# Two steps of the first expert group and the last block's sums taken into the group's switch

## The chip, the cores and the metric

The kernel runs on one core of one Trainium2 chip. The core has five engines with instruction streams of their own: TensorE (PE in the profile, with its weight loads as PEld), VectorE (DVE), ScalarE (ACT), GpSimd (POOL) and SyncE (SP, which only issues transfers). Matrix products read SBUF and write PSUM; the other engines read PSUM and write SBUF; transfers between device memory and SBUF go through 16 DMA engines. Instructions of an engine run in their order; engines wait for each other by semaphores. The metric is the device time of one execution in microseconds (us).

## The reference

It is an attention layer followed by a layer of experts, all in float32. The attention has 4 sequences of 768 tokens, 8 heads of 64. A query sees the first 8 keys and the last 96, with a bias that falls with distance. Each of the 3072 tokens of 512 values then goes to one of 8 experts:

```python
logits = x @ w_gate
expert_idx = np.argmax(logits, axis=1)
...
for e in range(E):
    mask = expert_idx == e
    xe = x[mask]
    h = np.maximum(xe @ w1[e], 0.0)     # 512 -> 1024
    ye = h @ w2[e]                      # 1024 -> 512
    out[mask] = gate_w[mask, None] * ye
```

How many tokens an expert gets depends on the data.

## The kernel before, in words

The kernel has two stages. **Attention** goes through 24 blocks of 128 queries (`steps(n)`, N = 24). It is pipelined over blocks: the step of block n computes its scores, while the values of block n-1, the sums (softmax denominators and gate logits) of block n-2 and the final rows of block n-3 are made. So the last blocks leave a tail behind the loop: `values_part(N)` and `sums_part(N)`, and then `sums_part(N + 1)` for the last block of all. A `sums_part` is 12 small products (L571), four transposes (L578), a copy on ACT (L573) and one more transpose (L581). The rows of the tokens, with gate and number, are scattered by GpSimd into device memory, sorted by expert.

**Experts**: the groups run in the order 0, E, 1, 2, ... 7. Group 0 is expert 0 with the tokens of the first three sequences only, so that it can start before the last sequence is routed; group E holds expert 0's tokens of the last sequence, computed by plain products (L1026). A group reads its tokens in two halves (even and odd slots) and multiplies in Winograd's way: seven products of quarter size in place of eight, as seven steps. The up product has two such sevens (`ups`, 14 steps), the down product one. Sums of quarters are made by DVE ahead (`x_sums`, L847 to L850, `w_sums`, `h_sums`) and behind each step (for example L915). A float32 product appears in the profile as two weight loads and two passes (MATMUL).

The number of columns of the products depends on how many tokens the group has. `SIZES` lists the column counts for which code exists, up to 256. `tables` compares the group's count with the list and leaves an index in SBUF. TensorE's code for a group stands once for every entry of the list (a form); the other engines' code stands once. Three things choose the form:

TensorE's code is brought by DMA (queue q8 in the profile).

Everything is recorded in program order by `Flow`, which works out the semaphores; no scheduler moves instructions later. In a group's code, `run(steps, first)` calls the steps and, after step i, what `at_(i, ...)` has put there for the other engines. In group 0, `ups[:1]`, `sums_part(N + 1)` and `ups[1:2]` are recorded ahead of `with f.forms(...)`, so they stand once, with 256 columns; from `ups[2:]` on everything is within the forms. The form's index for group 0 is loaded in the last attention step (L1239), ahead of the last transpose of its sums; the hint is recorded after the loop (L1322).

## Time and profile before

| What | us |
|---|---|
| Time, median of 3 runs (496.9 to 499.92) | 497.37 |
| The profiled execution, its own time | 498.01 |
| Its span, first to last instruction | 496.1 |
| TensorE busy, products | 473.4 |
| DVE busy | 355.8 |
| Hint of group 0, last instruction | 158.8 |
| Branch into group 0's form | 165.9 |
| Branch out of it | 196.3 |
| Branch into group 1's form | 217.2 |

The last four rows are moments from the span's start. The span is what the profile covers; 1.9 us of the execution lie outside it. Busy times are sums over the span and overlap between engines. In the profile's rows, a line number is the kernel's line that issued the instruction; "128x176" behind a product of L883 means 128 partitions and 176 columns. The granted clock of TensorE was full from 6.9 us to the end of the work (mean 0.989).

### The profile page before, as it was taken

Reading aid. Unit: us, or ns where it says so; the run is one execution under the profiler, and the core shown is the slowest. Engines: PE = TensorE matmul, PEld = TensorE weight load, DVE = VectorE, ACT = ScalarE, POOL = GpSimd, SP = SyncE. Lnnn points to the kernel's source line nnn. Section 1 sums busy time; section 2 is a strip of 40 time slices with the busy share of each in tenths; the row PEclk is TensorE's granted clock in tenths of the full one; section 3 lists DMA queues with packets and bytes.
Section 4 is the critical chain, followed back from the end, with each engine's and each line's share of the span. In section 5 each row is a group of like instructions: output and inputs, shape, how many; then the busy total and the mean of one; then the engine's idle time right before and its main releaser. Section 6 shows DMA issues by size and latency. Waiting matters only on the chain. (4 is left out here: it accounts for less than half of the span.)

```text
span 496.1 us, 10821 instructions
## 1 busy us (share of the span) xinstructions
PE 473.4 (95%) x4413; PEld 447.9 (90%) x4413; DVE 355.8 (72%) x638; ACT 172.4 (35%) x309; POOL 166.4 (34%) x196
## 2 busy tenths in 40 slices
PE   7999999999998999999999999999999999999990
PEld 7888878887886899899999999999999999999980
DVE  6466777897876884666777886768877776787850
ACT  5665555644654230322114213204214203303410
POOL 2653578567775053302104213204304303003011
PEclk9999999999999999999999999999999999999995
DMA  9999999988624437999808918826936853701000
GB/s 175 216 249 263 194 235 265 251 205 190 153 88 86 171 131 164 204 223 213 187 6 206 286 32 218 235 52 161 269 84 161 256 112 115 210 1 49 21 24 30
DMA packets 120093, 79.26 MB, mean 160 GB/s; under 512 B 86170, under 2 KB 103066, under 8 KB 120020
## 3 DMA queue, kind: packets, MB, share of 16 engines
q1 hardware_dynamic: 112482, 63.52, 57.6%
q0 software_dynamic: 6480, 14.45, 8.2%
q8 instruction: 52, 0.85, 0.8%
q10 hardware_dynamic: 1058, 0.26, 0.3%
q14 instruction: 21, 0.17, 0.1%
HBM read 61.39 MB, written 23.71 MB: 172 GB/s over the span
## 5 line engine op out<-in xcount | busy, mean ns | idle before, releaser
L883 PE MATMUL psum<-arena 128*128 128x208 f32 (+8 forms) x1760 | 286.2, 324 | 0.6 <-DVE arena L915 0.5
L883 PEld LDWEIGHTS psum<-arena 128*128 128x128 f32 x1760 | 280.8, 190 | 2.2 <-issue 0.9
L873 POOL DMA_INDIRECT out_dram<-arena,to x16 | 22.4, 1402 | 169.4 <-ACT arena L867 146.3
L529 DVE TENSOR_TENSOR arena<-psum,arena 128x1024 f32<-128x1024 f32 x40 | 48.4, 1219 | 30.5 <-PE psum L519 30.5
L537 ACT ACTIVATE arena<-arena 128x1024 f32<-128x1024 f32 (+1 forms) x48 | 47.5, 989 | 47.4 <-DVE arena L529 38.4
L543 POOL TENSOR_TENSOR arena<-arena 128x512 f32<-128x512 f32 x40 | 51.8, 1298 | 30.3 <-ACT arena L537 30.0
L907 ACT ACTIVATE arena<-arena 128x512 f32<-128x512 f32 x48 | 30.2, 630 | 61.2 <-DVE arena L939 25.4
L519 PE MATMUL psum<-arena 64*128 64x128 f32 x704 | 46.4, 280 | 1.8 <-ACT arena L505 1.8
L519 PEld LDWEIGHTS psum<-arena 64*128 64x128 f32 x704 | 41.8, 187 | 5.4 <-issue 2.5
L556 PE MATMUL psum<-arena 128*64 128x128 f32 x704 | 43.7, 276 | 0.4 <-issue 0.4
L911 ACT COPY arena<-psum 128x512 f32<-128x512 f32 (+1 forms) x24 | 13.5, 560 | 81.4 <-PE psum L883 81.3
L556 PEld LDWEIGHTS psum<-arena 128*64 128x64 f32 x704 | 37.9, 137 | 3.0 <-issue 0.8
L790 POOL DMA_INDIRECT xg_dram<-small,pad x24 | 23.4, 975 | 50.0 <-ACT arena L920 39.1
L655 POOL DMA_INDIRECT xg_dram<-arena,slot_i x24 | 24.4, 1017 | 21.5 <-DVE arena L978 16.0
L939 DVE TENSOR_TENSOR arena<-arena,psum 128x512 f32<-128x512 f32 x24 | 16.5, 688 | 16.4 <-PE psum L883 13.7
L926 DVE TENSOR_TENSOR arena<-arena,psum 128x512 f32<-128x512 f32 x23 | 15.8, 688 | 17.0 <-PE psum L883 16.2
L978 DVE TENSOR_TENSOR arena<-arena,psum 128x512 f32<-128x512 f32 x23 | 15.8, 688 | 15.4 <-PE psum L883 13.5
L944 DVE TENSOR_TENSOR arena<-arena,psum 128x512 f32<-128x512 f32 x24 | 16.5, 689 | 14.1 <-PE psum L883 12.0
L873 POOL DMA_INDIRECT out_dram<-ylast,to x17 | 17.0, 1001 | 22.0 <-ACT ylast L867 13.9
L739 DVE TENSOR_TENSOR arena<-arena 128x1024 f32<-128x1024 f32 x16 | 20.3, 1266 | 2.8 <-DMA arena<-in_moe_w_dram 2.8
L915 DVE TENSOR_TENSOR arena<-arena,psum 128x512 f32<-128x512 f32 (+1 forms) x24 | 15.8, 656 | 8.3 <-PE psum L883 7.9
L742 DVE TENSOR_TENSOR arena<-arena 128x1024 f32<-128x1024 f32 x16 | 19.5, 1221 | 1.7 <-issue 1.5
(164 smaller groups left out, 551.9 us busy)
## 6 DMA issues: line engine op xcount, KB each, us to landing
arena<-in_moe_w_dram SPq DMA_DIRECT2D x64, 512.0 KB
arena<-xg_dram SPq DMA_DIRECT2D x64, 128.0 KB
arena<-in_v_dram SPq DMA_DIRECT2D x24, 256.0 KB
arena<-in_q_dram SPq DMA_DIRECT2D x23, 256.0 KB
arena<-in_k_dram SPq DMA_DIRECT2D x23, 256.0 KB
xg_dram<-arena SPq DMA_DIRECT2D x2, 1032.0 KB
xg_dram<-arena,slot_i POOLq DMA_INDIRECT x24, 5.9
xg_dram<-small,pad POOLq DMA_INDIRECT x24, 8.7
```

Source lines behind the costliest of these rows:

```text
L519: f.pe.matmul(self.psum[:, 2 * g + a, c:c + P], lhsT=kt[r, m, :], rhs=qt[r, m, :], start=True, stop=True, skip_group_check=True)
L529: f.dve.tensor_tensor(e, s, self.bias[:, g, :, 1:3, :].rearrange("p h k c -> p h (k c)"), ALU.add)
L537: f.act.activation(e, e, AF.Exp)
L543: f.pool.tensor_tensor(self.es[n % 3][:, g], e[:, :, 0:P], e[:, :, P:2 * P], ALU.add)
L556: f.pe.matmul(po[r, m, :], lhsT=self.v[(n - ab) % 6][:, 2 * m + a, :], rhs=self.e[n % 2][:, m // 2, 2 * a + m % 2, P * ab:P * ab + P], sta ...
L655: self.f.pool.indirect_dma_start(out=self.xs[:], out_offset=bass.IndirectOffsetOnAxis(ap=k["slot_i"][:, b % 2, u:u + 1], axis=0), in_=self ...
L739: return [lambda: V.tensor_tensor(c["t3"], c["b22"], c["b12"], ALU.subtract), lambda: V.tensor_tensor(c["t1"], c["b12"], c["b11"], ALU.sub ...
L742: lambda: V.tensor_tensor(c["t4"], c["b21"], c["t2"], ALU.subtract)]
L790: self.f.pool.indirect_dma_start(out=self.xs[:], out_offset=bass.IndirectOffsetOnAxis(ap=self.keep["pad"][:, g, j:j + 1], axis=0), in_=sel ...
L873: return pool.indirect_dma_start(out=self.out[:], out_offset=bass.IndirectOffsetOnAxis(ap=self.keep["to"][:, g, j:j + 1], axis=0), in_=sel ...
L883: f.pe.matmul(self.psum[:, bank, 256 * t + cut.start:256 * t + cut.stop], lhsT=w[k][:, ts(t, 128)], rhs=x[k][:, cut], start=(fresh and t = ...
L907: f.act.activation(d, d, act)
```

## The change

Three edits:

1. The list of sizes: steps of 2 columns begin at 160 instead of 168, and between 208 and 256 there are 220, 232 and 244. That makes 37 forms instead of 32.
2. The first two up steps of group 0 and, between them, the last block's `sums_part(N + 1)` are recorded within the group's forms. The two steps then have the form's column count instead of 256, and the branch comes before them. Each of the 37 bodies of group 0 holds the 12 products and five transposes of the sums and the 8 products of the two steps.
3. The hint for group 0 stands in the last attention step, in the place of the load, and does the load itself (L79: where no load was recorded, it records one). TensorE's order there was load, transpose (L581), hint; it is load, hint, transpose.

```diff
-    RUNS = (range(128, 168, 4), range(168, 208, 2), range(208, 256, 48))
+    RUNS = (range(128, 160, 4), range(160, 208, 2), range(208, 256, 12))
...
             if n == N - 1:
-                f.load(*forms[0])
+                f.hint(*forms[0])
             at.both(n, 0)
...
         assert not numbers and not w0 and not w0_sums and not scat
-        f.hint(*forms[0])
         at.normal(N - 3, U)
...
             if g == 0:
 
-                run(ups[:1], 0)
-                sums_part(N + 1)
-                run(ups[1:2], 1)
                 pieces = ex.w_pieces(1)
...
             with f.forms(*forms[g]):
+                if p == 0:
+                    run(ups[:1], 0)
+                    sums_part(N + 1)
+                    run(ups[1:2], 1)
                 run(ups[2:], 2)
```

## The prediction

> **What bounds the kernel now.** I read the page's busy shares first, then TensorE's products kept apart by shape, then the order of time around the first expert group, then what TensorE's sequencer does there, last the DMA.

> ```profile
> PE 473.4 (95%) x4413; PEld 447.9 (90%) x4413; DVE 355.8 (72%) x638; ACT 172.4 (35%) x309; POOL 166.4 (34%) x196
> ```
> TensorE (PE) works 473.4 of 496.1 us, so whatever shortens or stops its stream moves the end almost one to one; the chain of work that ended last covers only the final 3 us and does not help.

> ```profile
> L883 PE MATMUL psum<-arena 128*128 128x176 f32 x192 | 29.3, 313 | 0.0
> ...
> L883 PE MATMUL psum<-arena 128*128 128x256 f32 x16 | 3.9, 386 | 0.0
> ```
> These are group 0's products: 192 passes at the count that its form chose (176 columns) and only 16 at the full 256. The 16 are the two steps that the change moves.

> ```profile
> 162.13 0.29 PE L581 MATMUL psum<-ident,arena 128*128 128x128 f32 x1
> 162.26 1.89 PE L883 MATMUL psum<-arena 128*128 128x256 f32 x8
> ...
> 164.87 0.69 DVE L848 TENSOR_TENSOR arena<-arena 128x512 f32<-128x512 f32 x1
> ...
> 165.61 4.38 PE L883 MATMUL psum<-arena 128*128 128x256 f32 x24
> ...
> 179.83 19.26 PE L883 MATMUL psum<-arena 128*128 128x176 f32 x128
> ```
> Step one runs from 162.26, step two from 165.61, just after DVE's L848 has made the sum that it reads (165.56). Passes follow each other at (1.89-0.38)/7 = 0.216 us at 256 columns and (19.26-0.31)/127 = 0.149 us at 176.

> ```profile
> L277 PEldq COMPARE_BRANCH  x16: 297/310/642, 165.9 to 482.4; - x16
> ```
> ```profile
> q8 instruction: 52, 0.85, 0.8%
> ```
> ```profile
> 199.00:202.00 3.00, 2.66 (x23) 2.26 (x22) 0.69 (x1) 2.27 (x4) 0.91 (x1) 1.00 1.06 265
> ```
> The first row is the branch into and out of the forms (sixteen, shortest, median and longest in ns). The first branch into a form is at 165.9, behind eight 256-column passes that are queued, so its 0.34 us and the 0.4 us around it cost nothing. Queue q8 brings TensorE's code, 52 packets of 16 KB. The last row (window, then busy time of the five engines, granted clock, DMA share, GB/s): around 200 us the DMA engines are full (share 1.06), which matters below.

> **What it removes.** Two steps of 8 passes go from 0.216 to 0.149 us each: 16 x 0.067 = 1.07 us less. Nothing else of TensorE's work changes: the counts that the other groups run (208, 182, 200, 184, 206, 198, 136) all stand in the new list of 37; the new 220, 232 and 244 are not used. DVE's table (L775) grows from 31 to 36 entries a group: 35 elements more in the larger call, a few hundredths beside products.

> **What it adds at the entry.** The branch now comes right after the transpose at 162.13, with no queue of work behind which to hide. Even with its code present, its sequence took 165.63 to 166.40 before the next product; that would put step one at about 163.1 instead of 162.26, a loss of 0.84.

> But is the code there? The trace's q8 packets here start at 148.80, 159.34, 162.53, 169.07, 183.28 and 201.61 us. From 124.20 to 159.34 TensorE went through 1025 instructions in four packets: 256 a packet. [...] The 159.34 packet belongs to the stream itself: between the third and the fourth of the hint's instructions lies a gap of 0.22 us where 0.06 is usual, so a block ends there, and the next is asked for. The hint ends at 158.89, and its target comes as the next packet, at 162.53, 3.2 us behind (in groups 2 to 7, too, the hint's packet follows the one before by 3.1 to 3.7 us[...]). DMA was idle (0.01 in 157.0 to 162.3), so this isn't contention. When is a block usable? In groups 5 and 7 the branch took 0.62 and 0.64 us instead of 0.31 to 0.41; it ended 1.35 and 1.34 us after its packet did. So here: 162.53 + 1.22 (the packet) + 1.35 = 165.10. Before, the branch came at 165.90 and found it; now it comes at about 162.4 and waits.

> The move of the hint doesn't help: it passes one transpose only (two instructions), the load of its index starts at 157.33 as before, and the block ends at the same place in the stream, now just ahead of the hint itself. The transpose of 158.20 is held behind six hint instructions until about 158.9; DVE's chain (L590 at 158.57, busy without a break up to 166.7) starts 0.7 us later, so L848 ends at 166.26. That would hold step two if the branch were quick; with the stall step two is later than that, and it is covered.

> Sum: first load 0.15 us after the branch (group 7), its product 0.13 later: 165.38, against 162.26: +3.12. The shorter steps give back 1.07, DVE's wait ahead of step two (165.37 to 165.61) another 0.21. Step three begins at 169.28 instead of 167.44: **+1.84 us**. Bounds: the block usable 0.25 sooner or later, 1.6 to 2.1.

> What is queued behind the waiting branch: all of TensorE; ACT's copies; the last block's DVE chain (L590 at 168.25) and with it the scatters on POOL; on SP the four w2 loads (L722 at 165.56) that wait for the last transposes and now go at about 168.2. They serve expert 1's second half, more than 50 us on. SP's loads at 186 to 204 move with the chain.

> **What it adds at the exit.** A product in float32 is two loads and two passes. Group 0's body before: 104 x 4 + 12 bf16 products x 2 + hint + exit branch = 442 instructions, two blocks. Now 8 more products (32), 12 sums (48), 5 transposes (10): 532, three blocks, the third holding 20 instructions. The trace shows that the exit's block is asked for only when the stream enters the block that holds the exit: the 183.28 packet comes with 223 of the body's instructions begun and 34 queued ahead, at number 257, 13 us ahead of the exit branch (196.26). Now this point is number 512. It is passed when 478 have begun, 54 instructions or 27 passes x 0.149 = 4.0 us before the body's end (198.78 + 1.84 = 200.62), at 196.6. From there 0.7 us to the packet (groups 2 to 7 show 0.71 to 0.76 after the entry branch), 1.15 for it and 1.35 until usable: 199.8 if DMA is free, in time. It isn't free: after the old exit (196.57) the next packet began at 201.61, 4.3 us later than 0.7 would give. With that row, usable at 204.1, first load 204.3: **+3.7 us**. Bounds: 0 without contention; 5.1 with the 5.7 that the body packets of groups 2 to 4 lag (some 72 instructions, 36 passes x 0.16, past number 256). I take 3.7, the nearest row in time and load.

> **The clock.** TensorE would stand idle twice for 2.9 and 3.7 us. The granted clock was halved at 484.7, 1.85 us after the last product (482.88), so an idle stretch of this length may halve it. [...] At the start the clock rose 5.4 us after the first product; half of that, 2.7 us a gap, is the upper bound, 0 the lower. I take 0.5 in all[...].

> Total: 1.84 + 3.7 + 0.5 = +6.0. The profiled execution (498.01 us, span 496.1 and 1.9 around it) would be 504.0; the median of the runs, 497.37, becomes **503.4 us**.

> **Rivals.** (1) Not slower. One mechanism: the code for the body arrives by 162.4, because the hint, now at the block's edge, replaces the fetch of 159.34 rather than queueing behind it (159.34 + 0.9 + 1.35 = 161.6). From that point the branch costs only its own 0.84, and L848's 166.26 sets step two: step three at 167.51 instead of 167.44. With the exit hidden too this is 497.4; if DVE's chain is less late, 496.9. [...] Against: in before the hint came 0.2 us after the edge and lost. (2) Entry stall alone, exit hidden behind the 34 queued instructions: +1.84, 499.2. For: free DMA would be in time; against: share 0.98 to 1.14 from 190 to 208. (3) Exit stall alone: 501.1. (4) Both gaps halve the clock at full price: up to 508, the tail.

> **How the numbers follow.** Forecast (both stalls, clock somewhere) 0.56, its own range 500.9 to 506.5; entry alone 0.17; exit alone 0.09; neither 0.14; over 506.5 0.04. The range 498.0 to 506.5 leaves out the case of neither and the tail. About 1% (5.0 us, 502.3) is what a measurement of this kernel tells from no change; the forecast lies just past it. Slower by over 1%: three quarters of the forecast, a fifth of exit alone and the tail, 0.48; faster 0.02; the rest, 0.50, within.

> **What would show it.** Right: the first branch into a form at about 162.4, lasting some 2.7 us; 208 passes at 176 and none at 256 columns; step three about 1.8 us later than 167.44; a code packet more in group 0; an exit branch of several us near 198, with TensorE idle before L861's first transposes; everything behind shifted alike. Wrong: entry branch at 0.3 to 0.4 us (rival 1), or exit at 0.3 us (rival 2), or the shift lost again at a later DMA wait of DVE's (L739 waits 2.8 us in all).

## The result, and the profile after

The kernel after takes 504.37 us, the median of six executions (501.58 to 510.35); the kernel before, timed on the same chip, 497.31 (496.79 to 499.92). The ratio is 1.0127, with an interval of 1.0097 to 1.0157: slower by 1.3%. (A ratio leaves out executions more than 1.5% above their kernel's fastest, here that of 510.35, so it isn't the quotient of the medians beside it.) The forecast was 503.4. The six executions fall into two groups, 501.58, 501.86, 502.73 and 506.01, 508.40, 510.35. The profiled one took 502.73 (span 500.8), so it belongs to the quick group and shows 4.7 us of loss where the medians differ by 7.

The page after, busy time and the queue of TensorE's code; then TensorE's products by shape:

```profile
PE 474.0 (95%) x4413; PEld 448.7 (90%) x4413; DVE 360.1 (72%) x638; ACT 172.3 (34%) x309; POOL 166.8 (33%) x196
...
q8 instruction: 53, 0.87, 0.8%
```
```profile
L883 PE MATMUL psum<-arena 128*128 128x176 f32 x208 | 32.0, 314 | 0.7 <-issue 0.5 <-DVE arena L848 0.2
```

The row had 192 passes before; the 16 of the two moved steps have joined it, none with 256 columns is left, and there is one packet of code more. Yet PE's busy time rose by 0.6 us although 16 passes became shorter: other passes became longer (L861's from 17.8 to 19.4 us in all, L1026's from 14.6 to 15.6). The order of time around the entry (start, length, line, product, count, and in brackets the idle time ahead of it and who ended it):

```profile
162.24 1.45 PE L883 MATMUL psum<-arena 128*128 128x176 f32 x8 [0.53 <-issue]
...
165.39 3.85 PE L883 MATMUL psum<-arena 128*128 128x176 f32 x24 [0.19 <-DVE arena L848]
```

There is no stall at the entry. The branch began at 161.65 and took 0.44 us; one packet of code came between the hint (ended at 157.94) and the branch, at 158.96, one microsecond behind the hint. Step one takes 1.45 us in place of 1.89. Measured from the load of the index (156.55 now, 157.33 before), step one starts 0.76 us later than before, step two 0.56, and the step behind both still 0.02 (166.69 now, 167.44 before). So what the shorter passes give is used up even where nothing stalls: the transpose behind the hint starts 1.44 us after the load in place of 0.88, the branch has no queued work to hide behind, and step two waits for DVE's sum. The exit is different. First the sixteen branches (shortest, median, longest in ns), then the order of time behind the body:

```profile
L277 PEldq COMPARE_BRANCH  x16: 292/350/6149, 161.7 to 487.2; - x16
```
```profile
201.71 3.86 PE L861 MATMUL psum<-ident,arena 128*128 128x128 f32 x16 [3.38 <-DVE arena L739]
...
211.80 0.27 PE L1308 MATMUL psum<-ident,ok 128*1 128x128 f32 x1
```

The longest branch, 6.15 us, is group 0's exit: it began at 195.51 with 34 instructions queued ahead, the last pass started at 198.02, and TensorE stood for 3.38 us. The row names DVE's L739, but such names are inferred, and the branch fits better: it ended at 201.66, 0.05 us ahead of L861, and the last packet of code before that, of 199.15, took 1.13 us. The same two products before:

```profile
198.93 1.04 PE L861 MATMUL psum<-ident,arena 128*128 128x128 f32 x8
...
207.24 0.27 PE L1308 MATMUL psum<-ident,ok 128*1 128x128 f32 x1 [0.34 <-DVE ok L1303]
```

L861's products start 2.78 us later than there, or 3.56 measured from the load. Last, two windows of after (window, length, busy PE, PEld, DVE, ACT, POOL, granted clock, DMA share, GB/s):

```profile
199.00:202.00 3.00, 0.29 (x2) 0.29 (x3) 2.00 (x3) 0.00 (x0) 0.00 (x0) 0.80 1.11 265
202.00:205.00 3.00, 3.00 (x15) 2.54 (x15) 2.52 (x6) 1.61 (x3) 0.61 (x1) 0.50 0.97 149
```

The clock was halved from 200.78 to 207.61. L1308, in group E, comes 4.56 us later than before where L861 came 2.78 later: the halved clock cost 1.78. The account of the 4.7 us of span: attention 0.78 quicker, the body's last pass 0.03 later measured from the load, exit +3.53, clock +1.78, later groups +0.15.

### The profile page after: what moved, and what is told of

The parts are those of the page before. It is cut to its first block, busy times and chain, and to the rows that moved or that the text cites. A ratio compares the mean times of both kernels' runs of the same rounds, so it can differ in the third digit from the quotient of the medians.

```text
span 500.8 us, 10821 instructions
## 1 busy us (share of the span) xinstructions
PE 474.0 (95%) x4413; PEld 448.7 (90%) x4413; DVE 360.1 (72%) x638; ACT 172.3 (34%) x309; POOL 166.8 (33%) x196
## 5 line engine op out<-in xcount | busy, mean ns | idle before, releaser
L883 PE MATMUL psum<-arena 128*128 128x176 f32 (+7 forms) x1760 | 285.3, 323 | 1.3 <-issue 0.5
L883 PEld LDWEIGHTS psum<-arena 128*128 128x128 f32 x1760 | 280.2, 190 | 3.0 <-issue 1.9
L556 PE MATMUL psum<-arena 128*64 128x128 f32 x704 | 43.7, 276 | 0.0
L556 PEld LDWEIGHTS psum<-arena 128*64 128x64 f32 x704 | 37.9, 137 | 2.6 <-issue 0.2
L944 DVE TENSOR_TENSOR arena<-arena,psum 128x512 f32<-128x512 f32 x24 | 16.5, 688 | 14.6 <-PE psum L883 14.5
L861 PE MATMUL psum<-ident,arena 128*128 128x128 f32 x132 | 19.4, 292 | 3.7 <-DVE arena L739 3.4
L740 DVE TENSOR_TENSOR arena<-arena 128x1024 f32<-128x1024 f32 x15 | 21.2, 1413 | 0.0
```

What stands on the lines that cost most here:

```text
L556: f.pe.matmul(po[r, m, :], lhsT=self.v[(n - ab) % 6][:, 2 * m + a, :], rhs=self.e[n % 2][:, m // 2, 2 * a + m % 2, P * ab:P * ab + P], sta ...
L740: lambda: V.tensor_tensor(c["t1"], c["b12"], c["b11"], ALU.subtract),
L861: self.f.pe.transpose(pt[:, c, :], self.yt[:, c, hh, ts(bb, 128)], self.keep["ident"][:])
L883: f.pe.matmul(self.psum[:, bank, 256 * t + cut.start:256 * t + cut.stop], lhsT=w[k][:, ts(t, 128)], rhs=x[k][:, cut], start=(fresh and t = ...
```

## The experiments

Ratios are to the kernel before, timed beside each set of kernels: 499.29 us beside e1 to e4, 498.59 beside e5 to e8, 499.66 beside e9 to e11 and 499.26 beside e12. Stretches within a kernel are from its one profiled execution.

The theory: code comes in blocks of 256 instructions, an estimate from the packets (in after, 1028 instructions of TensorE began in the four packets' time from 123.41 to 158.96), and what decides is where a branch stands in its block. Blocks and edges below are counts by that estimate; no trace shows what a packet holds. By the theory the exit stalls because the stream enters the third block 20 instructions ahead of the exit branch, while DMA is full (share 1.06 in 196 to 199).

**Is it the third block? e4: the kernel before, with its body padded** to 532 instructions by 45 tiny products. Nothing of the change is in it.

```diff
+def pad():
+    pr, oh = psum[:, U, 384:392], keep["oh"][:, 0, :]
+    for _ in range(45):
+        f.pe.matmul(pr, lhsT=before[:], rhs=oh, start=True, stop=True, skip_group_check=True)
...
-at_(4, lambda: at.counts(U, whole), lambda: at.gates(B - 1, whole))
+at_(4, pad, lambda: at.counts(U, whole), lambda: at.gates(B - 1, whole))
```

> The kernel before, with nothing changed but 45 small products (8 columns, bf16) ahead of the counts in group 0's body, whose results the counts overwrite: the body grows from 442 to 532 instructions, as in the change. Theory: the exit stalls as in the change, +3.7 and about +1.6 from the halved clock, and the products cost 45 x 0.025 = 1.1: 503.7 (501 to 507), exit branch 4 to 7 us. Rival (moving the steps and sums is what costs): 497.3 + 1.1 = 498.4, exit branch 0.3 us.

Measured: 503.79 us, ratio 1.0096 (1.0066 to 1.0126). Its branches, and the first work behind the exit:

```profile
L277 PEldq COMPARE_BRANCH  x16: 292/320/6171, 166.0 to 487.8; - x16
```
```profile
203.69 3.50 PE L861 MATMUL psum<-ident,arena 128*128 128x128 f32 x16 [3.40 <-DVE arena L739]
```

6.17 and 3.40 us, as in after (6.15 and 3.38), without any edit of the change: the length of the body alone makes the exit's stall. The body's place in the program does not show in it: counted through the whole program, the exit stands 8 instructions behind a multiple of 256 in e4, 174 in e1 and 214 in after, and its branch took 6.17, 6.26 and 6.15 us.

**Two blocks again, e3**: the change with the last down step of group 0 outside the forms; the body has 500 instructions.

```diff
-run(ex.down(g, (lambda: [...]) if early else None), D)
+downs = ex.down(g, (lambda: [...]) if early else None)
+run(downs[:-1] if p == 0 else downs, D)
+    if p == 0:                      # behind the forms
+        run(downs[-1:], D + 6)
```

> The change with the last step of group 0's down product behind its forms, at 256 columns: the body has 500 instructions, two blocks. Theory: the exit's code is asked for at instruction 256, 13 us ahead; exit branch 0.3 us, no halved clock; the last step costs 16 x 0.067 = 1.07 more. 497.3 + 0 at the entry + 1.07 = 498.4 (497.4 to 499.2). Rival (the loss comes from the move of the sums and the branch, or from transfers that start earlier): still about 504 + 1.

Measured: 510.33 us, ratio 1.023 (1.0187 to 1.0273), 12 us over the expectation. The exit branch took 0.32 us as expected. But group 1's branch into its form, 0.31 us before, took 4.26:

```profile
202.66 1.04 PE L861 MATMUL psum<-ident,arena 128*128 128x128 f32 x8
...
225.76 6.51 PE L883 MATMUL psum<-arena 128*128 128x208 f32 x26 [2.00 <-issue]
```

No idle time ahead of L861, but 2.00 us ahead of group 1's products, and the clock halved for 3.41 us behind it. Thirty-seven bodies that are each 32 instructions shorter shift the code of all later groups by a number that isn't a multiple of 256. Counted through the program, an edge now fell 61 instructions ahead of group 1's branch (189 in the change, 115 in the kernel before), and a packet came at 222.73, behind the branch's start of 221.3. Attention ends 2.6 us later than in before, with waits for the loads of q and k, which the edit doesn't touch. The profiled execution is the quickest of the four (506.03); what the others lost, 4 to 7 us more, no profile shows. So an edit of a form's length also moves every later branch against the edges, and with the exit's stall gone (0.32 us) another stood in the next group (4.26). That the edge made this one is argued from its place, not shown by a run of its own.

**How far ahead, and how full? e5**: the change with the same padding, so that the exit stands 110 instructions into its third block instead of 20.

> The change with 45 tiny products (8 columns, bfloat16, 90 instructions) added to group 0's body ahead of the counts; the body grows from 532 to 622 instructions and its exit from 20 to 110 instructions into the third block. Theory (the exit's block is asked for only when the stream enters the block that holds the exit, and 20 instructions were too few to hide a fetch): now some 10 us lie between, the exit branch takes about 0.3 us, TensorE doesn't idle ahead of L861, and the clock isn't halved there; against the change's quick executions -5.3 us for the exit and its clock, +1.1 for the products, so about 0.3 us over the kernel before, 4 to 6 more in executions in which the entry stalls. Rival (a third block costs a stall wherever the exit stands, or the stall is the cost of leaving a long body): exit still 6 us, total 5 to 6 us over the kernel before.

Measured: 503.79 us (499.39 to 509.11), ratio 1.0072 (1.0045 to 1.01). The profiled execution took 503.16; its entry and what follows the exit:

```profile
166.19 1.86 PE L883 MATMUL psum<-arena 128*128 128x176 f32 x8 [3.43 <-DVE arena L847]
...
204.33 1.04 PE L861 MATMUL psum<-ident,arena 128*128 128x128 f32 x8
```

The exit branch took 2.01 us, not 0.3, but it started 34 queued instructions ahead of the body's end and was over at 203.68, before the last pass started (204.18). So TensorE did not stand and the clock was not halved: the exit costs nothing. The quickest executions, 499.4, are 0.8 over the kernel before; the padding alone is 1.1 (by the end of e4's body, from the load). The rival, any third block costs, falls. The 3.43 us at the entry are the stall that the prediction described and that the profiled execution of the change did not have; the clock was halved behind it (the row's eight passes took 1.86 us, 1.45 in after).

**e6** moves expert 1's first four w1 loads (2 MB) behind the gathers on SP.

```diff
 ex.load_x(E, last)
+ex.load_x(1, last)
 for fn in pieces[:4]:
     fn()
-ex.load_x(1, last)
```

> The change with expert 1's first four w1 loads on SP put behind the gathers of its tokens instead of ahead of them. Theory (the 4.3 us in the exit's packet are the DMA engines, full with these loads): if the loads leave the stretch 196 to 201, the packet comes 1 to 3 us sooner and the exit branch takes 2 to 5 us instead of 6.1; if other transfers fill the stretch, the DMA share there stays at 1.0 and the branch at 6. Rival (the delay is the fetch's own, not contention): 6 us with a DMA share well below 1.

Measured, one execution: 505.06 us.

```profile
203.33 1.09 PE L861 MATMUL psum<-ident,arena 128*128 128x128 f32 x8 [1.68 <-DVE arena L978]
...
214.46 0.27 PE L1308 MATMUL psum<-ident,ok 128*1 128x128 f32 x1 [3.10 <-DVE ok L1303]
```

The exit branch took 4.45 us instead of 6.15. Its packet came 1.85 us after the branch's start; in after, e1, e2, e4 and e7 it came 3.6 to 3.9 after it. So with this order of the transfers the packet came at least 1.75 us sooner after the branch's start. That the w1 loads are the cause is likely but not shown: in seven kernels (after, e1, e2, e4, e7, e9, e10) the exit's packet starts 0.15 to 0.82 us after the last of their 512 packets (in after 199.15 after 198.84), but in e5 and e6 it comes in their midst, and in e6 they run from 196.97 to 209.05, through the fetch. DMA stayed busy (share 1.43 in 196 to 198, 0.84 in 198 to 200), so what the exit costs with idle DMA isn't shown. Nor is the kernel quicker: attention ends 3.3 us later than in after, and L1308 waits 3.10 us, because DVE waits for the moved loads.

**The entry. e1** is the change with the list of 32 sizes as before; **e2** is the change with load and hint back in their old places. The diffs are the change's own lines for `RUNS`, and for `f.load` and `f.hint`, reversed.

> The change with the old list of 32 sizes. Theory (the exit branch of group 0 stands in the first 20 instructions of a third block of code, which is asked for late and while DMA is full): the list plays no part; exit branch of group 0 4 to 7 us, clock halved for some us behind it, 504 us (501.5 to 508). Rival (the longer list, with more code and a larger table, costs): back near 497.5.

> The change with load and hint in their old places (load, transpose, hint). Theory: the hint is then two instructions later, behind the edge of a block again, so that the stream's own next block is fetched first (packet near 158.5 to 159.5) and the form's 3.2 us behind it; the entry branch, at about 161.7, waits until about 164.4 and takes 2.5 to 3 us instead of 0.44. With the exit stall as in the change: about 2 us more than it, 506. Rival (the code is there by 162 wherever the hint stands): entry branch 0.4 us, time as the change, 504.

Measured: e1 508.14 us (504.61 to 511.64), ratio 1.0143 (1.0078 to 1.0209); e2 509.61 (509.10 to 513.60), ratio 1.0198 (1.0165 to 1.0232). In both profiled executions the entry stalls, and the exit as well (6.26 and 6.37 us). e1's first product:

```profile
167.60 2.71 PE L883 MATMUL psum<-arena 128*128 128x176 f32 x8 [3.73 <-DVE arena L848]
```

The entry branch took 3.64 us in e1, 3.50 in e2, 3.34 in e5, and 0.43 or 0.44 in after, e3, e6 and e10, with the hint, by the count, one to three instructions behind the block's edge in all seven profiled executions. In the three that stall, the last packet of code ahead of the branch's end starts 1.0 to 1.1 us after the branch does; that it holds the form's code, asked for only when it was missed, is inferred from its time. In the four others a packet follows the hint itself by a microsecond. In the trace of before, two packets came ahead of the branch, at 159.34 and at 162.53; in e4, whose code up to this branch is that of before, with the hint at the same moment (158.75, 158.84 in before), one packet alone came, at 159.89, and the branch took 0.34. The busy share of the DMA engines in tenths, from 158 to 162 us in slices of 0.1 us, first of before, then of e4:

```profile
DMA  0000000000000500000000000000000000000000
```
```profile
DMA  0000000000000000005000000000000000000000
```

So the packets differ between executions of the same code, two in the one and one in the other. That the stream's own next block and the hint's target change places in them is the author's reading.

e1 and e2 also lost at a place that no theory had named: group 5's branch took 3.58 and 3.02 us. By the count, an edge lies 9 and 29 instructions ahead of it there; with 29 it took 0.83 us in after.

**Does the hint's place settle the entry? e7** puts the hint at the head of attention's last step. **e9** puts it behind that step's products of values (L556), and uses a list of 33 sizes by which no later group has an edge less than 109 instructions ahead of its branch; **e10** is e9 with the hint where the change has it. The edits of e9:

```diff
     values_part(n)
+    if n == N - 1:
+        f.hint(*forms[0])
...
-if n == N - 1:
-    f.hint(*forms[0])
...
-RUNS = (range(128, 160, 4), range(160, 208, 2), range(208, 256, 12))
+RUNS = (range(132, 168, 4), range(168, 208, 2), range(208, 256, 16))
```

> The change with its hint at the head of attention's last step, 60 instructions or more before the code block that holds the branch, not one instruction behind that block's edge. Theory (at the edge the hint races with the stream's own request for its next block, and the change's times fall into two groups by who wins): with the hint known before the edge the form's block is always the first that is asked for; entry branch 0.3 to 0.5 us, all executions within about 1.5 us, at 4 to 5 us over the kernel before, all of it from the exit (6.1 us, clock halved behind it). Rival (the two groups of times come from the exit or the DMA): still two groups, 4 to 5 and 9 to 13 us over the kernel before.

> The change with two edits. The hint stands behind the last step's products of values, some 56 instructions ahead of the edge of the block that holds the branch, where the sequencer has 34 instructions in hand (at the head of the step TensorE stood 1.1 us for it). The list has 33 sizes (132 to 168 by 4, to 208 by 2, 208, 224, 240, 256), so that in no later group an edge lies less than 100 instructions ahead of a branch into the forms. Theory (the entry is a race at the edge, the exit a late fetch): entry branch 0.3 to 0.5 us always, no stall in groups 1 to 7, exit branch about 6 us with the clock halved behind it; median 4 to 5.5 us over the kernel before, and a spread no wider than that kernel's own, 4 us. Rival (the spread of the change comes from elsewhere): executions 9 us or more over the kernel before remain.

> The same with the hint where the change has it, one instruction behind the edge; nothing else differs from the run with the early hint. Theory: the entry stalls in a part of the executions, 3 us and up to 1.7 for the halved clock each time; the quickest equal the quickest with the early hint, the median lies 1 to 4 us above it. Rival (the place of the hint is nothing): the same median within 1 us.

Measured: e7 508.25 us (505.46 to 510.12), ratio 1.017 (1.0133 to 1.0206); e9 501.96 (501.37 to 505.96), 1.0046 (1.0026 to 1.0066); e10 502.64 (501.36 to 507.93), 1.0063 (1.0038 to 1.0088). e7's profile shows two losses of its own making or luck:

```profile
154.56 3.28 PE L519 MATMUL psum<-arena 64*128 64x128 f32 x32 [1.11 <-issue]
...
384.36 4.98 PE L883 MATMUL psum<-arena 128*128 128x206 f32 x19 [2.54 <-issue]
```

At the head of the step nothing is queued to cover load and hint (1.4 us of TensorE's sequencer), and the clock was halved there (the row's 32 passes took 3.28 us, 2.06 in after); and group 5's branch, again 29 instructions behind an edge, took 3.24, although its hint had been known ahead of the edge: against the theory's "always". Its entry branch took 0.34, with a packet of code at 161.00, before the branch at 165.6. In e9 the hint costs 0.2 us, and entry and exit are those of the change:

```profile
165.61 1.45 PE L883 MATMUL psum<-arena 128*128 128x176 f32 x8 [0.43 <-issue]
...
205.26 1.09 PE L861 MATMUL psum<-ident,arena 128*128 128x128 f32 x8 [3.46 <-DVE arena L739]
```

e9's median is 2.3 us over the kernel before, not 4 to 5.5. e9 and e10 differ by 0.7 us in the median, inside the rival's bound: that an early hint helps in the timed executions is not shown. By their times, one execution of e10's fifteen (507.93) would fit a stalled entry, and most did not stall. The quickest of both, 501.4, stand 4.1 over the quickest of the kernel before beside them (497.2), which the exit and its clock would explain. That kernel itself ranged to 505.76. In e9's profiled execution (505.96) attention waits 5.8 us for the loads of q and k, so a part of the spread has nothing to do with the forms.

**A version of the idea that fits. e8 and e11** leave step one ahead of the forms at 256 columns, take only the sums and step two in, and make the counts with fewer products, so that the body stays within two blocks. e8: 7 count products, 40 sizes, hint at the head of the step, body 506. e11: 9 count products, the list of 33, the hint behind the products of values, body 510.

```diff
+if p == 0:
+    run(ups[:1], 0)
 with f.forms(*forms[g]):
     if p == 0:
-        run(ups[:1], 0)
         sums_part(N + 1)
         run(ups[1:2], 1)
```

> Step one stays ahead of the forms at 256 columns; the sums and step two move into them; the counts use 7 products instead of 12, so that the body has 506 instructions and fits two blocks; the hint stands at the head of attention's last step; 40 sizes (120 to 160 by 4, to 208 by 2, to 256 by 10), so that no edge of a code block lies between hint and branch in groups 1 to 7. Theory (code blocks decide): every branch 0.3 to 0.7 us, no stall and no halved clock; step two saves 0.54 us and five products of the counts about 0.3, so 0.3 to 1.0 us under the kernel before (-0.1 to -0.2%). Rival (the longer form body or the larger list costs time by itself): 2 us or more over the kernel before.

> Step one ahead of the forms at 256 columns, the sums and step two within them, counts in 9 products instead of 12, body 510 instructions (two blocks), the hint behind the last step's products of values, 33 sizes, so that group 1's branch lies 155 instructions behind an edge that follows its hint and no other group has an edge between hint and branch. Theory (code blocks decide): no branch over 0.7 us, no halved clock, 0.1 to 0.8 us under the kernel before. Rival (the moved step costs by itself): 1 us or more over it.

Measured: e8 499.76 us (497.78 to 504.65), ratio 1.0026 (1.0006 to 1.0046); e11 496.16 (495.89 to 500.08), ratio 0.9942 (0.9918 to 0.9965), the only kernel of all that is quicker than the kernel before. In e8 group 1's branch took 2.54 us: its hint came 49 instructions behind an edge, and of two packets the second, by its place the form's, came late (213.29, then 220.74), with DMA full from 216 on (share 1.03); most of that hid behind queued products (0.23 us idle). The hint at the head of the step cost TensorE 1.20 us (1.11 in e7), more than the 0.3 to 1.0 that e8 was to gain. In e11 the hint, by the count, precedes the edge. Its branches and its first two steps:

```profile
L277 PEldq COMPARE_BRANCH  x16: 294/302/889, 161.3 to 481.1; - x16
```
```profile
161.06 1.94 PE L884 MATMUL psum<-arena 128*128 128x256 f32 x8
...
164.90 3.85 PE L884 MATMUL psum<-arena 128*128 128x176 f32 x24 [0.39 <-DVE arena L849]
```

No branch above 0.89 us (0.7 was expected at most), and the clock full to the end of the work. Step two with the two steps behind it in its row takes 3.85 us where before took 4.38: 0.53.

**e12** takes only the hint's new place to the kernel before, to see what of e11's gain that is.

> The kernel before with nothing but its load and hint put behind the last step's products of values, where the sequencer has 34 instructions in hand; list, body and forms are the old ones. It tells which part of the 1.4 us (profiled executions) that the run with one placed step gained over the kernel before is the hint's place. Theory: the load and hint held TensorE 0.7 us between two transposes of attention's last step and the products behind; in the new place 0.2 us; so 0.4 to 0.8 us under the kernel before, step two's 0.5 us remaining for the moved step. Rival (the gain is all in the moved step and its placing): within 0.2 us of the kernel before.

Measured: 499.20 us (497.86 to 502.75), ratio 0.9996 (0.998 to 1.0013): nothing.

```profile
161.73 1.93 PE L883 MATMUL psum<-arena 128*128 128x256 f32 x8
165.57 4.38 PE L883 MATMUL psum<-arena 128*128 128x256 f32 x24 [0.39 <-DVE arena L848]
```

Step one comes 0.53 us sooner than in before (162.26), and step two at the same time (165.61 there): TensorE now waits 0.39 us for the sum that DVE makes (L848). What the hint gave, DVE's chain took back. By this the hint alone is no part of e11's gain; its list and its three products less in the counts were not timed alone. The profiled executions of e11 and before differ by 1.4 us at the last exit: 0.53 is step two, some 0.6 a shorter wait in attention for DVE's L599 (0.35 against 0.94) that nothing here explains. The quickest executions of the two differ by as much (495.89 and 497.22). The ratio says 2.9 us (1.7 to 4.1); how much of that is the spread of the kernel before is not settled.

## Why the prediction was right, and where not

The forecast of 503.4 us is 1 us from the median, and slower by just over 1% is what it leant to. The exit was foreseen rightly; the closeness of the sum is luck. Its steps:

**The removal, right.** Sixteen passes went to 176 columns; step one 1.89 to 1.45 us, step two's row 4.38 to 3.85: 0.97 against the 1.07 expected. The table's two calls (L775) took 0.04 us more.

**The entry, wrong as a certainty.** The step that failed is "The 159.34 packet belongs to the stream itself ... the block ends at the same place in the stream, now just ahead of the hint itself". By the count the edge is where it was said to be, but that the stream's packet comes before the hint's was read from a single execution. The profiled execution of the change does not show it: one packet, and 0.44 us at the branch. That is rival 1's entry, with step three +0.07 us by its sum and +0.02 measured, set by DVE's sum as that rival said. In three of seven profiled executions with the hint at the edge it stalled, for 3.34 to 3.64 us (the step said some 2.7), and a packet came about 1.0 us after the branch began, not 3.2 us after the packet ahead, as in before. Whether the three executions of the change at 506 to 510 are stalled entries, a stalled group 5 (3.0 to 3.6 us in e1, e2 and e7) or attention's loads stays open; none of them was profiled.

**The exit, right.** The argument by blocks (442 to 532 instructions, the third holding 20) and its size: 3.7 us predicted from the row of 201.61, 3.53 measured, and 3.4 us of idle time in the unchanged kernel with a padded body (e4). The cover of 4.0 us did not suffice with DMA full (share 1.06); in e6, with another order of the transfers, the packet came 1.85 us behind the branch's start in place of 3.6 to 3.9. (The upper bound of 5.1 counts the 0.7 us to the packet twice: a lag of 5.7 in all gives 4.4.) What the step did not see is that the longer body times 37 also moves every later branch against the edges. In after all later groups together cost only 0.15 us; in e3 TensorE stood 2.00 us at group 1's branch, and the clock was halved for 3.41.

**The clock, under-sized.** I took 0.5 us in all, an estimate that no row of before showed, against the row of 1.85 us. It cost 1.78 in the profiled execution: one gap of 3.38 us, halved for 6.83. Where it lasted 3.41 us (e1, e2, e4, e7, e9, e10) it cost 0.4 to 1.1, by the time from L861 to L1308. Gaps of 2.00 (e3), 2.33 (e2) and 2.54 us (e7) also halved it, gaps of 1.68 and 3.10 (e6) and 2.71 (e1) did not. So the length of one gap does not tell.

**The chances.** Both stalls had 0.56. In the profiled execution it was the exit alone, 501.1 predicted for the median; with the clock's 1.78 on top that is 502.9, just above the quick group. The number for the median came out close because an entry too dear by 1.8 us stood against a clock too cheap by 1.3 and against losses in half of the executions that the profile doesn't show.

## What to carry to other kernels

Where code stands once for each of many shapes, count its instructions before moving work into it: 20 instructions past a multiple of 256 cost more here (5.3 us with the clock) than the shorter steps could give (1.1). Cut the body back to the boundary or leave a step outside, as e11 did, and then look where the blocks' edges fall ahead of every later branch, since the count of copies times the length shifts them all (in e3, with a multiple of 256 now 61 instructions ahead of it, group 1's branch took 4.26 us). And the packets that one trace shows (two ahead of the branch in before) need not come so in the next execution (one in e4): give a step that rests on their order both outcomes.

## What the runs showed of the hardware

- An entry branch that stood until a packet of code came took 3.3 to 3.6 us: about 1 us to the packet, 0.9 to 1.2 for it, and 1.42 or 1.43 until the branch ends (e1, e2, e5). With the DMA engines busy (share 0.84 to 1.22), branches took 4.3 to 6.4 (e3, e6, and the exits). The last part is nearly the same for group 0's exit in after (199.15 + 1.13 = 200.28; the branch ended at 201.66, 1.38 later) and for the entries of groups 5 and 7 before (1.35 and 1.34).
- A hint alone did not settle what its branch took. By the count of 256 one to three instructions behind an edge, it stood ahead of branches of 0.43 or 0.44 us and of 3.3 to 3.6. Known 39 instructions ahead of an edge, with the branch 29 behind it (group 5), it stood ahead of branches of 0.54 to 0.83 us (after, e6) and of 3.0 to 3.2 (e2, e7). Over the 98 branches into groups 1 to 7 of the fourteen profiled kernels, 17 have an edge 9 to 61 instructions ahead: four took 3.0 to 4.3 us, thirteen 0.39 to 1.09. Of the other 81, two took over 1 us (1.93 in e1, 2.54 in e8). So a near edge did not decide it.
- In e7 the clock was halved at 155.14 behind two gaps of 0.94 and 1.11 us within 3 us, with no longer one near; in e6 a gap of 3.10 us, ahead of 214.46, did not halve it.
- Between the start and the end of the work, halved stretches lasted 3.41 or 6.83 us in all these kernels.
